# Splitting x and inverting row sums: high parts a step ahead of low parts, in a fused attention and two-MoE kernel

## The chip, the cores and the metric

The kernel runs on one core of a Trainium2 chip. The metric is the device time of one execution in microseconds (us), lower is better.

## The reference, cut to what matters

```python
def _attn_ref(q, k, v):               # B, H, S, D = 4, 8, 576, 64
    scores = scale * np.matmul(q, k.transpose(0, 1, 3, 2))
    ...
    scores = np.where(mask, scores + bias[None], -1000000000.0)   # causal, window 128
    scores = scores - np.max(scores, axis=-1, keepdims=True)
    attn = np.exp(scores)
    attn = attn / (np.sum(attn, axis=-1, keepdims=True) + 1e-09)
    return np.matmul(attn, v)

def _moe_ref(x, w_in, w_out):         # 2304 tokens, 512 -> 2048 -> 512
    h = x @ w_in
    g = h * np.cos(h)
    return g @ w_out

def _moe2_ref(x, w_in, w_out):
    h = x @ w_in
    g = np.where(h >= 1, h, np.where(h <= -1, 0.0, (h + 1) ** 2 / 4))
    return g @ w_out
```

The output of attention is x of the first MoE layer, and its output is x of the second.

## The kernel before, in words

Three stages follow one another: attention, then the first MoE layer over four chunks of tokens, then the second over five. The matmuls of the MoE layers run on pairs of numbers: every fp32 value is held as a rounded high part (a cast to fp32r, on ACT) and a low part (value minus high part, `sub_lo`, on DVE or POOL), and each product is three matmuls: high by high, low by high, high by low.

**Attention** works on 36 pairs, one for every 256 tokens and two heads. A pair has two blocks j of 128 tokens. For a pair, `pe_s` (L236) puts the scores of both blocks into the PSUM banks y0 to y3; `scores` (L253) adds the distances and takes the row minimum on DVE (L263) and the exponentials with their sums on ACT (L270); `prepare` (L445) adds 1e-9 to the sums on POOL and `invert` (L448) takes their reciprocals on DVE, or does both on DVE with `add=True`; `normalise` (L273) multiplies on POOL; `pe_t` (L280) transposes on PE into banks h0 and h1; `copy_t` (L293) copies each bank to SBUF, on DVE or ACT by the table `PT`; `pe_v` (L304) multiplies by v into bank h2 or h3; `put_x` (L319) takes the result out as part of x.

The loop of `attention` (L464) is a software pipeline. Step k emits `pe_s` and `scores` of pair k+3, inverts pair k+2, normalises pair k+1 (in the steps below 1 it normalises pair k+2 at once), transposes and copies pair k, and takes out pair k-1. The order on PE, DVE, ACT, POOL and SP is the order in which the code emits; nothing reorders it, so a waiting instruction holds up all that stands behind it on its engine. Behind the loop the last five pairs, p0 to p4 (pairs 31 to 35), are written out by hand, and then the first MoE layer starts with `mm_a` (L360).

Some work of the MoE layer lies in the attention stage. `make(0)` (L169) emits one of the small pieces that turn 64-bit weights into fp32 and split them (L114, L125, L131, L135, L140 and an L81); nine of them go into the steps in `D_STEPS`, five behind p4's copies. The first chunk's x has two parts. Its second part, tokens 512 to 767 (pairs 8 to 11, taken out in steps 9 to 12), is split straight from PSUM in `put_x`:

```python
            ACT.copy(hi, p["vb"][:, 0:256])
            sub_lo(DVE, lo, p["vb"][:, 0:256], hi)
```

Its first part, tokens 0 to 511, four tiles x0 to x3 of 128 x 512, is split by `split_x` (L347) late in the stage: x0 in step 30, x1 in step 31, x2 and x3 among the hand-written last pairs. Slots for x come from a list of 17 (L194): `new_x` takes the one that has been free the longest, `free_x` puts one back. The low parts xl of x0 to x3 lie where the distances of the four head pairs lie during attention. In a profile all low parts have the line of `sub_lo`, L81.

Of the kernel before, what the change touches and what calls it, by code (L numbers as in the profile page):

```python
# [10 lines left out]
F32R = mybir.dt.float32r  # L11
# [32 lines left out]
def attention_moe_moe_kernel(  # L44
# [9 lines left out]
    ACT, DVE, POOL, PE, SP = nc.scalar, nc.vector, nc.gpsimd, nc.tensor, nc.sync  # L54
# [15 lines left out]
    def nm(s):  # L70
        uid[0] += 1
        return f"{s}{uid[0]}"

    def small(name, dtype=F32, shape=(128, 512)):
        return two.tile(list(shape), dtype, tag="s", name=nm(name), bufs=12)

    def f32(ap):
        return ap.bitcast(F32)

    def sub_lo(eng, out, full, hi):  # L80
        eng.tensor_tensor(out=out, in0=full, in1=f32(hi), op=ALU.subtract)  # L81
# [81 lines left out]
    def start(m):  # L163

        if not started[m]:
            started[m] = True
            next(making[m])

    def make(m):  # L169

        start(m)
        if next(making[m], making) is not making:
            made[m] += 1
# [19 lines left out]
    x_tiles = {}  # L193
    x_free = {512: list(range(17)), 256: list(range(4))}  # L194

    def new_x(w, dtype=F32):
        size = w if x_free[w] else 512
        slot = size, x_free[size].pop(0)
        return one.tile([128, size], dtype, tag=f"x{size}.{slot[1]}", name=nm("x"))[:, 0:w], slot

    def free_x(slot):
        x_free[slot[0]].append(slot[1])
# [3 lines left out]
    def x_lo(n):  # L206

        return one.tile([128, 512 if n < 4 else 256], F32R, tag=f"xl{n}", name=nm("xl"))
# [17 lines left out]
    def load(n, part=slice(0, 1024)):  # L226
        if n < len(pairs):
            p = pairs[n]
            if "ld" not in p:
                p["ld"] = ring.tile([128, 1024], F32, tag="wl" if n % 2 else "wh", name=nm("qkv"))  # L230
                p["left"] = [0, 1024]
            if part.start >= p["left"][0] and p["left"][0] < 1024:
                p["left"][0] = part.stop
                SP.dma_start(p["ld"][:, part], qkv[p["b0"] // 2, p["hp"], :, part])
# [38 lines left out]
    def normalise(p):  # L273
        for j in range(2):
            st, sc, w = p["st"], p["sc"][j], p["w"][j]
            POOL.tensor_tensor(  # L276
                out=sc[:, :, 0:w], in0=sc[:, :, 0:w],
                in1=st[:, 8 + 2 * j:10 + 2 * j].unsqueeze(2).to_broadcast([128, 2, w]), op=ALU.mult)

    def pe_t(p):  # L280
        p["tb"], p["pt"] = [], [None] * 2
        for j in range(2):
            nb = p["w"][j] // 128
            b = ps.tile([128, 512], F32, tag=f"h{j}", name=nm("pa"))
            for h in range(2):
                for i in range(nb):
                    c = (h * nb + i) * 128
                    PE.transpose(b[:, c:c + 128], p["sc"][j][:, h, i * 128:i * 128 + 128], ident)  # L288
            p["tb"].append(b)
# [3 lines left out]
    def copy_t(p, j, eng=None):  # L293
        p["pt"][j] = pt = small("pt")
        n = 2 * p["w"][j]
        if (eng or PT[copies[0] % len(PT)]) == "A":
            ACT.copy(pt[:, 0:n], p["tb"][j][:, 0:n])
        else:
            DVE.tensor_copy(pt[:, 0:n], p["tb"][j][:, 0:n])
        copies[0] += 1  # L300
# [3 lines left out]
    def pe_v(p):  # L304
        v_no[0] += 1
        p["vb"] = b = ps.tile([128, 512], F32, tag=f"h{2 + v_no[0] % 2}", name=nm("pa"))
        for j in range(2):
            nb = p["w"][j] // 128
            for i in range(nb):
                for h in range(2):  # L310
                    vc = 640 + (j + 2 - nb + i) * 128 + 64 * h
                    c = (h * nb + i) * 128
                    PE.matmul(b[64 * h:64 * h + 64, j * 128:j * 128 + 128],  # L313
                              lhsT=p["ld"][:, vc:vc + 64], rhs=p["pt"][j][:, c:c + 128],
                              start=(i == 0), stop=(i == nb - 1))

    evicted = [0]

    def put_x(p, eng=None):  # L319
        t0 = p["b0"] * 128  # L320
        o, w = max(a for a in all_parts if a[0] <= t0)
        if (o, w) == chunks[0]["parts"][1]:
            hi, slot = new_x(w, F32R)
            lo = x_lo(4 + p["hp"])
            chunks[0]["xs", 1, p["hp"]] = hi, lo, slot
            ACT.copy(hi, p["vb"][:, 0:256])
            sub_lo(DVE, lo, p["vb"][:, 0:256], hi)
            return
        if (o, p["hp"]) not in x_tiles:
            x_tiles[o, p["hp"]] = new_x(w)  # L330
        x = x_tiles[o, p["hp"]][0][:, t0 - o:t0 - o + 256]
        if (eng or XE[evicted[0] % len(XE)]) == "A":
            ACT.copy(x, p["vb"][:, 0:256])
        else:
            DVE.tensor_copy(x, p["vb"][:, 0:256])
        evicted[0] += 1
# [8 lines left out]
            free_x(c["xs", i, d][2])  # L345

    def split_x(c, i, ds):  # L347
        o, w = c["parts"][i]
        for d in ds:
            x, slot = x_tiles.pop((o, d))  # L350
            hi, hi_slot = new_x(w, F32R)
            lo = x_lo(4 * i + d)[:, 0:w]
            ACT.copy(hi, x)
            sub_lo(DVE, lo, x, hi)
            free_x(slot)
            c["xs", i, d] = hi, lo, hi_slot

    h_no = [-1]

# [85 lines left out]
    def prepare(p):  # L445
        POOL.tensor_scalar_add(p["st"][:, 4:8], p["st"][:, 4:8], 1e-9)

    def invert(p, add=False):  # L448
        if add:
            DVE.tensor_scalar_add(p["st"][:, 4:8], p["st"][:, 4:8], 1e-9)  # L450
        DVE.reciprocal(p["st"][:, 8:12], p["st"][:, 4:8])  # L451

    def attention():
        qk, v = slice(0, 640), slice(640, 1024)
        for part in (qk, v):
            for n in range(3):
                load(n, part)
        make_identity(nc, ident)
        make_dist8()
        DVE.memset(half, 0.5)  # L460
        DVE.memset(half_pi, TWO_PI / 4)
        np_ = len(pairs)
        c0 = chunks[0]
        for k in range(-AHEAD, np_ - AHEAD - 1):  # L464
            new = pairs[k + AHEAD]
            mid = pairs[k + AHEAD - 1] if k + AHEAD >= 1 else None
            nrm = pairs[k + AHEAD - 2] if k >= 2 else None
            cur = pairs[k] if k >= 0 else None
            old = pairs[k - 1] if k >= 1 else None
            if k > -AHEAD:  # L470
                load(k + AHEAD + 1)
                load(k + AHEAD + 2)
            if k == 0:
                pe_t(cur)
            pe_s(new)
            if k > 0:
                pe_t(cur)
            if old:
                pe_v(old)
            scores(new, 0)  # L480
            if k < 1 and mid:

                prepare(mid)
                invert(mid)
                normalise(mid)
            if cur:
                copy_t(cur, 0)
            if nrm:
                normalise(nrm)
            if k >= 1:  # L490
                prepare(mid)
            scores(new, 1)

            if k in D_STEPS:
                make(0)
            if k in (np_ - 6, np_ - 5):
                split_x(c0, 0, [k - (np_ - 6)])
            if k >= 1:
                invert(mid)
            if cur:  # L500
                copy_t(cur, 1)
            if k + 1 == D_STEPS[0]:
                start(0)
            if old:
                put_x(old)

        p0, p1, p2, p3, p4 = pairs[np_ - 5:]
        pe_s(p4)
        pe_t(p1)
        pe_v(p0)  # L510
        scores(p4, 0)
        copy_t(p1, 0, "D")
        normalise(p2)
        invert(p3, add=True)
        normalise(p3)
        copy_t(p1, 1, "A")
        scores(p4, 1)
        pe_t(p2)
        pe_v(p1)
        copy_t(p2, 0, "D")  # L520

        ACT.activation(half_pi2, half, AF.Sin)
        put_x(p0, "A")
        invert(p4, add=True)
        normalise(p4)
        copy_t(p2, 1, "D")
        pe_t(p3)
        pe_v(p2)
        split_x(c0, 0, [2])
        put_x(p1, "D")  # L530
        copy_t(p3, 0, "D")
        copy_t(p3, 1, "A")
        pe_t(p4)
        pe_v(p3)
        put_x(p2, "A")
        split_x(c0, 0, [3])
        copy_t(p4, 0, "D")
        copy_t(p4, 1, "A")
        make(0)
        make(0)  # L540
        pe_v(p4)
        put_x(p3, "A")
        for _ in range(D_TAIL - 2):
            make(0)
        put_x(p4, "A")
# [115 lines left out]
```

## Time and profile before

| what | value |
|---|---|
| median of 3 runs | 930.52 us (930.34 to 932.04) |
| the profiled execution, its own time | 930.21 us |
| its span, first to last instruction | 928.4 us |
| PE busy | 909.6 us (98%) |
| DVE, ACT, POOL busy | 551.6 (59%), 435.2 (47%), 120.8 us (13%) |
| chain that ended last | PE 79%, DVE 10%, ACT 8%, issue 2% |
| granted TensorE clock | 0.999 |
| start of the first MoE matmul | 127.84 us |

How to read it: the span is that of one profiled execution; 1.8 us of that execution's own time lie outside it. PE is busy 98% of the span, but this is a mean over an attention stage of 128 us and MoE stages of 800 us. The chain that ended last is followed back from the last instruction to whatever released each step; where it passes through DVE or ACT, PE was waiting for them.

### The profile page before, as it was taken

Reading aid. Unit: us, or ns where it says so; the run is one execution under the profiler, and the core shown is the slowest. Engines: PE = TensorE matmul, PEld = TensorE weight load, DVE = VectorE, ACT = ScalarE, POOL = GpSimd, SP = SyncE. Lnnn points to the kernel's source line nnn. Section 1 sums busy time; section 2 is a strip of 40 time slices with the busy share of each in tenths; the row PEclk is TensorE's granted clock in tenths of the full one; section 3 lists DMA queues with packets and bytes.
Section 4 is the critical chain, followed back from the end, with each engine's and each line's share of the span. In section 5 each row is a group of like instructions: output and inputs, shape, how many; then the busy total and the mean of one; then the engine's idle time right before and its main releaser. Section 6 shows DMA issues by size and latency. Waiting matters only on the chain.

```text
span 928.4 us, 13106 instructions
## 1 busy us (share of the span) xinstructions
PE 909.6 (98%) x4944; PEld 755.2 (81%) x4944; DVE 551.6 (59%) x1192; ACT 435.2 (47%) x923; POOL 120.8 (13%) x147
## 2 busy tenths in 40 slices
PE   7999988999999999999999999999999999999998
PEld 5767777888888888888888888888888888888898
DVE  6888788888868667767433543344344334433443
ACT  7788865665655444444455532232233223322332
POOL 5666620000000000000144510000000000000000
PEclk9999999999999999999999999999999999999999
DMA  9346013333305443542322200010001000100100
GB/s 355 145 168 265 2 67 116 116 128 120 116 34 191 136 151 122 170 137 92 102 100 104 69 1 1 0 46 1 1 1 45 1 1 1 46 0 1 39 9 23
DMA packets 24687, 74.77 MB, mean 81 GB/s; under 512 B 2736, under 2 KB 3632, under 8 KB 24624
## 3 DMA queue, kind: packets, MB, share of 16 engines
q1 hardware_dynamic: 24624, 73.94, 22.9%
q8 instruction: 39, 0.64, 0.3%
q14 instruction: 24, 0.20, 0.1%
HBM read 60.82 MB, written 13.11 MB: 80 GB/s over the span
## 4 chain that ended last, share of the span: by engine, by line
PE 79%; DVE 10%; ACT 8%; issue 2%; POOL 0%; DMA 0%; ACTq 0%; DVEq 0%
PE y L425 36%; PE h L375 36%; PE pa L248 2%; PE pa L288 2%; PE pa L313 2%; DVE wu L131 2%; ACT t L391 2%; ACT sc L270 2%; DVE t L393 1%; ACT wh L140 1%; DVE wl L81 1%; DVE gl L81 1%; DVE wu L135 1%; ACT wu L114 1%; ACT gh L405 1%
## 5 line engine op out<-in xcount | busy, mean ns | idle before, releaser
L375 PE MATMUL h<-x,wh 128*128 128x512 f32 (+1 forms) x640 | 237.0, 370 | 1.0
L375 PE MATMUL h<-xl,wh 128*128 128x512 f32 (+1 forms) x640 | 235.6, 368 | 0.0
L375 PE MATMUL h<-x,wl 128*128 128x512 f32 (+1 forms) x640 | 235.5, 368 | 0.0
L425 PE MATMUL y<-gl,wh 128*128 128x512 f32 (+1 forms) x576 | 217.5, 378 | 0.4 <-DVE gl L81 0.4
L425 PE MATMUL y<-gh,wh 128*128 128x512 f32 (+1 forms) x576 | 217.3, 377 | 0.0
L425 PE MATMUL y<-gh,wl 128*128 128x512 f32 (+1 forms) x576 | 217.3, 377 | 0.0
L396 ACT ACTIVATE t<-t,half 128x512 f32<-128x512 f32 (+1 forms) x80 | 54.4, 680 | 189.7 <-DVE t L395 189.4
L375 PEld LDWEIGHTS h<-x,wh 128*128 128x128 f32 x640 | 120.6, 188 | 23.6 <-DVE t L393 3.2
L375 PEld LDWEIGHTS h<-x,wl 128*128 128x128 f32 x640 | 120.7, 189 | 20.3
L375 PEld LDWEIGHTS h<-xl,wh 128*128 128x128 f32 x640 | 120.6, 188 | 20.1
L81 DVE TENSOR_TENSOR gl<-t,gh 128x512 fp32r<-128x512 f32 (+1 forms) x144 | 95.5, 663 | 68.3 <-ACT gh L405 64.1
L405 ACT CAST gh<-t 128x512 fp32r<-128x512 f32 (+1 forms) x144 | 86.0, 597 | 105.0 <-DVE t L398 56.4
L425 PEld LDWEIGHTS y<-gl,wh 128*128 128x128 f32 x576 | 108.5, 188 | 21.0 <-DVE gl L81 1.1
L425 PEld LDWEIGHTS y<-gh,wh 128*128 128x128 f32 x576 | 108.4, 188 | 20.0
L425 PEld LDWEIGHTS y<-gh,wl 128*128 128x128 f32 x576 | 108.3, 188 | 19.9
L395 DVE TENSOR_SCALAR t<-h 128x512 f32<-128x512 f32 (+1 forms) x80 | 50.9, 636 | 88.9 <-PE h L375 88.8
L81 POOL TENSOR_TENSOR wl<-wst,wh 128x512 fp32r<-128x512 f32 x32 | 41.1, 1308 | 372.6 <-ACT wh L182 372.6
L398 DVE TENSOR_TENSOR t<-h,t 128x512 f32<-128x512 f32 (+1 forms) x80 | 51.1, 638 | 61.8 <-ACT t L396 61.8
L391 ACT ACTIVATE t<-t,half_pi 128x512 f32<-128x512 f32 x80 | 54.6, 682 | 62.6 <-DVE t L389 62.6
L389 DVE SCALAR_TENSOR_TENSOR t<-h,k 128x512 f32<-128x512 f32 x80 | 50.8, 635 | 54.6 <-ACT k L387 54.4
L270 ACT ACTIVATE sc<-sc,st 128x256 f32<-128x256 f32 (+1 forms) x144 | 70.2, 489 | 23.9 <-DVE st L263 20.5
L276 POOL TENSOR_TENSOR sc<-sc,st 128x512 f32<-128x512 f32 (+1 forms) x72 | 70.0, 994 | 35.3 <-DVE st L451 30.5
(56 smaller groups left out, 853.1 us busy)
## 6 DMA issues: line engine op xcount, KB each, us to landing
wst<-in_w SPq DMA_DIRECT2D x64, 512.0 KB, 3.7
qkv<-in_qkv SPq DMA_DIRECT2D x33, 512.0 KB, 9.4
wd<-wu SPq DMA_DIRECT2D x32, 256.0 KB, 2.4
wst<-wd SPq DMA_DIRECT2D x16, 512.0 KB, 3.3
out_t<-ys SPq DMA_DIRECT2D x16, 256.0 KB, 2.1
qkv<-in_qkv SPq DMA_DIRECT2D x3, 320.0 KB, 3.6
qkv<-in_qkv SPq DMA_DIRECT2D x3, 192.0 KB, 5.1
out_t<-ys SPq DMA_DIRECT2D x4, 128.0 KB, 1.8
```

The costliest lines, as they stand in the source:

```text
L81: eng.tensor_tensor(out=out, in0=full, in1=f32(hi), op=ALU.subtract)
L131: DVE.scalar_tensor_tensor(out=ui, in0=high, scalar=0x80000000, in1=ui, op0=ALU.bitwise_and, op1=ALU.bitwise_or)
L270: ACT.activation(sc[:, h, 0:w], sc[:, h, 0:w], AF.Exp, bias=st[:, c:c + 1], scale=-1.0, accum_out=st[:, 4 + c:5 + c])
L276: POOL.tensor_tensor(out=sc[:, :, 0:w], in0=sc[:, :, 0:w], in1=st[:, 8 + 2 * j:10 + 2 * j].unsqueeze(2).to_broadcast([128, 2, w]), op=ALU. ...
L375: PE.matmul(h, lhsT=a[:, 0, s], rhs=x, start=(n == 0), stop=(n == 11))
L389: DVE.scalar_tensor_tensor(out=t, in0=h, scalar=INV_2PI, in1=k, op0=ALU.mult, op1=ALU.subtract)
L391: ACT.activation(t, t, AF.Sin, bias=half_pi, scale=TWO_PI)
L395: DVE.tensor_scalar(out=t, in0=h, scalar1=-1.0, scalar2=1.0, op0=ALU.max, op1=ALU.min)
L396: ACT.activation(t, t, AF.Square, bias=half, scale=0.5)
L398: DVE.tensor_tensor(out=t, in0=h, in1=t, op=ALU.max)
L405: ACT.copy(gh, t)
L425: PE.matmul(c["y", i][d], lhsT=a[:, 1, s], rhs=x, start=(f == 0 and k == 0 and not (i and d % 2)), stop=(f == NF - 1 and k == 2 and (i == ...
```

## The change

Three edits. (1) In steps -2 to 0 the reciprocals of pairs 0 to 2 move from ahead of the second half of the new pair's scores to behind it; the addition of 1e-9 for them moves from POOL to DVE, and `normalise` follows there. (2) The low parts of pairs 8 to 11 are emitted on DVE one step later than the high parts on ACT, behind the next pair's scores. (3) x0, x1 and x2 get their high parts at the ends of steps 29, 30 and 31; the low parts of x0 and x1 follow in steps 30 and 31 behind the scores, and those of x2 and x3 move behind the copies of p4. One `make(0)` moves ahead of these copies.

```diff
--- before.py
+++ after.py
@@ -315,6 +315,7 @@
                               start=(i == 0), stop=(i == nb - 1))
 
     evicted = [0]
+    low_parts = []
 
     def put_x(p, eng=None):
         t0 = p["b0"] * 128
@@ -324,7 +325,7 @@
             lo = x_lo(4 + p["hp"])
             chunks[0]["xs", 1, p["hp"]] = hi, lo, slot
             ACT.copy(hi, p["vb"][:, 0:256])
-            sub_lo(DVE, lo, p["vb"][:, 0:256], hi)
+            low_parts.append(lambda: sub_lo(DVE, lo, p["vb"][:, 0:256], hi))
             return
         if (o, p["hp"]) not in x_tiles:
             x_tiles[o, p["hp"]] = new_x(w)
@@ -345,15 +346,23 @@
             free_x(c["xs", i, d][2])
 
     def split_x(c, i, ds):
+        for d in ds:
+            split_hi(c, i, d)()
+
+    def split_hi(c, i, d):
+
         o, w = c["parts"][i]
-        for d in ds:
-            x, slot = x_tiles.pop((o, d))
-            hi, hi_slot = new_x(w, F32R)
+        x, slot = x_tiles.pop((o, d))
+        hi, hi_slot = new_x(w, F32R)
+        ACT.copy(hi, x)
+
+        def rest():
             lo = x_lo(4 * i + d)[:, 0:w]
-            ACT.copy(hi, x)
             sub_lo(DVE, lo, x, hi)
             free_x(slot)
             c["xs", i, d] = hi, lo, hi_slot
+
+        return rest
 
     h_no = [-1]
 
@@ -478,11 +487,6 @@
             if old:
                 pe_v(old)
             scores(new, 0)
-            if k < 1 and mid:
-
-                prepare(mid)
-                invert(mid)
-                normalise(mid)
             if cur:
                 copy_t(cur, 0)
             if nrm:
@@ -493,17 +497,23 @@
 
             if k in D_STEPS:
                 make(0)
-            if k in (np_ - 6, np_ - 5):
-                split_x(c0, 0, [k - (np_ - 6)])
-            if k >= 1:
-                invert(mid)
+            while low_parts:
+                low_parts.pop()()
+            if mid:
+                invert(mid, add=k < 1)
+                if k < 1:
+
+                    normalise(mid)
             if cur:
                 copy_t(cur, 1)
             if k + 1 == D_STEPS[0]:
                 start(0)
             if old:
                 put_x(old)
-
+            if k >= np_ - 7:
+                low_parts.append(split_hi(c0, 0, k - (np_ - 7)))
+
+        x2, = low_parts
         p0, p1, p2, p3, p4 = pairs[np_ - 5:]
         pe_s(p4)
         pe_t(p1)
@@ -526,20 +536,21 @@
         copy_t(p2, 1, "D")
         pe_t(p3)
         pe_v(p2)
-        split_x(c0, 0, [2])
         put_x(p1, "D")
         copy_t(p3, 0, "D")
         copy_t(p3, 1, "A")
         pe_t(p4)
         pe_v(p3)
         put_x(p2, "A")
-        split_x(c0, 0, [3])
+        make(0)
         copy_t(p4, 0, "D")
         copy_t(p4, 1, "A")
+        x2()
+        pe_v(p4)
+        x3 = split_hi(c0, 0, 3)
+        put_x(p3, "A")
         make(0)
-        make(0)
-        pe_v(p4)
-        put_x(p3, "A")
+        x3()
         for _ in range(D_TAIL - 2):
             make(0)
         put_x(p4, "A")
```

On DVE at the program's start, steps -1 and 0 (`sc` are scores of a pair, `pa` the PSUM bank, `st` a pair's sums; `ISA` on sc is the addition with the row minimum, the row that follows reads its result), one piece of the difference:

```order
-L451 RECIPROCAL st_134<-st_134 128x4
-L263 ISA sc_177,st_159<-pa_164,xl_105 128x256
+L263 ISA sc_173,st_159<-pa_164,xl_105 128x256
 L263 ISA st_159 128x1
-L263 ISA sc_177,st_159<-pa_165,xl_105 128x256
+L263 ISA sc_173,st_159<-pa_165,xl_105 128x256
 L263 ISA st_159 128x1
+L459 TENSOR_SCALAR st_134<-st_134 128x4
+L460 RECIPROCAL st_134<-st_134 128x4
```

The reciprocal of the pair before (`st_134`) stood between the two halves of the next pair's scores; now both halves come first, then an addition, then the reciprocal.

On DVE around step 10 (`xl_674` is the low part of pair 8, `x_673` its high part from ACT, made at the end of step 9; `sc_707` here and `sc_716` below are scores of pair 13, `wu` a piece of weights), before:

```order
L131 SCALAR_TENSOR_TENSOR wu_355<-wst_353,wu_355 128x512
L451 RECIPROCAL st_573<-st_573 128x4
L81 TENSOR_TENSOR xl_674<-pa_645,x_673 128x256
L263 ISA sc_707,st_679<-pa_680,xl_102 128x256
L263 ISA st_679 128x1
```

and now:

```order
L263 ISA sc_716,st_678<-pa_684,xl_102 128x256
L263 ISA st_678 128x1
L81 TENSOR_TENSOR xl_674<-pa_645,x_673 128x256
L460 RECIPROCAL st_626<-st_626 128x4
L263 ISA sc_758,st_730<-pa_731,xl_105 128x256
```

The low part `xl_674` stood ahead of the first scores of pair 13 (`sc_707`); now it stands behind the last of them, ahead of the next reciprocal.

On DVE at the end of the stage, from the second copy of p2 on (`pt` are the copies of p2, p3 and p4, `xl` the low parts of x2 and x3, `wu` pieces of weights), before:

```order
L299 COPY pt_1876<-pa_1853 128x512
L81 TENSOR_TENSOR xl_1898<-x_357,x_1897 128x512
L335 COPY x_1692<-pa_1858 128x256
L299 COPY pt_1902<-pa_1878 128x512
L81 TENSOR_TENSOR xl_1927<-x_410,x_1926 128x512
L299 COPY pt_1930<-pa_1906 128x512
L131 SCALAR_TENSOR_TENSOR wu_1037<-wst_404,wu_1037 128x512
L135 SCALAR_TENSOR_TENSOR wu_1037<-wst_404,wu_1037 128x512
```

and now:

```order
L299 COPY pt_1878<-pa_1855 128x512
L336 COPY x_1692<-pa_1860 128x256
L299 COPY pt_1900<-pa_1880 128x512
L131 SCALAR_TENSOR_TENSOR wu_1037<-wst_404,wu_1037 128x512
L299 COPY pt_1925<-pa_1904 128x512
L81 TENSOR_TENSOR xl_1929<-x_357,x_1800 128x512
L135 SCALAR_TENSOR_TENSOR wu_1037<-wst_404,wu_1037 128x512
L81 TENSOR_TENSOR xl_1949<-x_410,x_1940 128x512
```

Ahead of the last copy two low parts are gone and one piece of weights has come; the low parts follow the last copy.

## Rows read from the trace of the kernel before

**Rows 1.** By stage: window, length, busy us of PE, PEld, DVE, ACT, POOL, clock, DMA, GB/s

```profile
127.84:150.00 22.16, 19.61 (x107) 16.62 (x106) 18.05 (x34) 12.92 (x26) 0.00 (x0) 1.00 0.35 119
```

**Rows 2.** Waits in 0 to 130 us: who waited for whom, us in total, times, longest

```profile
DVE xl L81 <- ACT x L326: 4.7, 4, 1.5
...
DVE xl L81 <- ACT x L353: 3.5, 3, 1.4
PE pa L288 <- DVE pt L299: 3.3, 3, 1.5
...
DVE st L451 <- POOL st L446: 2.7, 4, 1.0
```

**Rows 3.** Timeline at the start, PE: start us, duration, instruction xcount [idle before <- releaser]

```profile
9.39 0.66 PE L288 MATMUL pa<-ident,sc 128*128 128x128 f32 x4 [0.31 <-POOL sc L276]
...
12.78 1.04 PE L248 MATMUL pa<-qkv 64*128 64x256 f32 x4 [1.01 <-DVE st L263]
...
14.46 0.63 PE L288 MATMUL pa<-ident,sc 128*128 128x128 f32 x4 [0.28 <-ACT pt L297]
```

**Rows 4.** The same timeline, POOL

```profile
9.94 1.61 POOL L276 TENSOR_TENSOR sc<-sc,st 128x256 f32<-128x256 f32 x2 [0.30 <-DVE st L451]
11.64 0.22 POOL L446 TENSOR_SCALAR st<-st 128x4 f32<-128x4 f32 x1
```

**Rows 5.** The same timeline, DVE

```profile
11.89 0.18 DVE L451 RECIPROCAL st<-st 128x4 f32<-128x4 f32 x1 [0.88 <-POOL st L446]
...
12.30 0.41 DVE L263 CUSTOM_DVE_ANT_0 sc<-pa,xl 128x256 f32<-128x256 f32 x1
```

**Rows 6.** Timeline of steps 10 and 11, DVE: low parts of pairs 9 and 10

```profile
46.24 0.42 DVE L81 TENSOR_TENSOR xl<-pa,x 128x256 fp32r<-128x256 f32 x1 [1.46 <-ACT x L326]
...
50.81 0.42 DVE L81 TENSOR_TENSOR xl<-pa,x 128x256 fp32r<-128x256 f32 x1 [0.90 <-ACT x L326]
```

**Rows 7.** Timeline, PE: `pe_s` of pairs 13, 18 and 19

```profile
41.00 1.13 PE L248 MATMUL pa<-qkv 64*128 64x256 f32 x8
...
59.79 0.92 PE L248 MATMUL pa<-qkv 64*128 64x256 f32 x8
...
62.69 0.92 PE L248 MATMUL pa<-qkv 64*128 64x256 f32 x8
```

**Rows 8.** Timeline, PE: a full step (pairs 33, 30 and 29), then the end of attention

```profile
106.83 1.13 PE L248 MATMUL pa<-qkv 64*128 64x256 f32 x8
107.90 1.09 PE L288 MATMUL pa<-ident,sc 128*128 128x128 f32 x8
...
109.94 1.13 PE L248 MATMUL pa<-qkv 64*128 64x256 f32 x8
...
116.91 0.63 PE L288 MATMUL pa<-ident,sc 128*128 128x128 f32 x4 [1.49 <-DVE pt L299]
...
124.95 1.07 PE L288 MATMUL pa<-ident,sc 128*128 128x128 f32 x8 [1.46 <-DVE pt L299]
...
127.84 0.50 PE L375 MATMUL h<-x,wh 128*128 128x512 f32 x1
...
130.47 0.39 PE L375 MATMUL h<-x,wl 128*128 128x512 f32 x1
```

**Rows 9.** Timeline of the end, DVE

```profile
115.40 0.69 DVE L81 TENSOR_TENSOR xl<-x,x 128x512 fp32r<-128x512 f32 x1 [1.32 <-ACT x L353]
...
120.20 0.70 DVE L450 TENSOR_SCALAR st<-st 128x4 f32<-128x4 f32 x1 [0.28 <-ACT sc L270]
...
122.50 1.37 DVE L81 TENSOR_TENSOR xl<-x,x 128x512 fp32r<-128x512 f32 x1 [0.81 <-ACT x L353]
```

**Rows 10.** Timeline of the end, ACT

```profile
109.72 0.51 ACT L270 ACTIVATE sc<-sc,st 128x256 f32<-128x256 f32 x1 [0.53 <-DVE st L263]
...
110.72 0.60 ACT L353 CAST x<-x 128x512 fp32r<-128x512 f32 x1
```

**Rows 11.** Timeline of the end, POOL: the two halves of p4's `normalise`

```profile
121.28 2.04 POOL L276 TENSOR_TENSOR sc<-sc,st 128x512 f32<-128x512 f32 x2 [0.41 <-DVE st L451]
```

## The prediction

> **What bounds the kernel now.** First the table by stage. In the first 22 us of the MoE stage PE is busy 19.61 of 22.16 us [rows 1], and over the whole span 98%, so nearly all that attention loses, the kernel loses: what counts is how early the first MoE matmul, now at 127.84 us [rows 8], can start. The TensorE clock stands at its upper level throughout (granted 1.00 [rows 1]), so it is no term here. Next I read the PE timeline of attention for its undisturbed pace. A full step (`pe_s`, `pe_t`, `pe_v`) goes from 106.83 to 109.94, 3.11 us, without a wait of PE [rows 8]; one with a block of 128 keys goes from 59.79 to 62.69, 2.90 us [rows 7]. Third, the list of waits up to 130 us, for what breaks this pace [rows 2]: DVE waits 4.7 us, in four places, for the high parts of pairs 8 to 11; 3.5 us, in three, for those of x0, x1 and x2; 2.7 us, in four, for POOL's addition ahead of a reciprocal; PE waits 3.3 us, in three, for DVE copies. All are in-order waits: a DVE instruction stands at the head of its queue until ACT or POOL is done, with scores and copies ready behind it. Each of the three edits takes away one such group, so I cost three places.
>
> **Place one, the start.** In step 0 the reciprocal of pair 2 waits 0.88 us on DVE and starts at 11.89, since POOL's addition for it (11.64) stands behind a `normalise` of 1.61 us that began at 9.94 [rows 4, 5]. Behind it stand a copy and the second scores of pair 3 (12.30) [rows 5]; PE waits 1.01 us for these banks (12.78), then 0.28 us for ACT's copy (14.46) [rows 3], and from there runs at its pace. With the change those scores don't wait for POOL. The gain is at most the 1.01 us of PE's wait. Something comes off: the reciprocal of pair 0 now stands behind two scores (0.41 us each, overlapping [rows 5]), where it had waited anyway, and its `normalise`, on which PE waits 0.31 us at 9.39 [rows 3], comes about 0.2 us later. So 0.88 - 0.1 = **0.8 us**, nearest to the wait that goes. Bounds 0.4 and 1.0: the lower takes a further 0.4 us for an addition on DVE that meets a running `normalise`. The three new additions work on four numbers a partition (the one beside a running `normalise` took 0.70 us [rows 9]), and three on POOL go.
>
> On that price a row and a rule meet. The addition at 120.20 took 0.70 us, and the low part of x2 at 122.50 took 1.37 against 0.69 for that of x1 [rows 9], which began when POOL was idle; POOL's `normalise` ran from 121.28 to 123.32 [rows 11]. The Trainium skill (SBUF — State Buffer, "Who interferes with whom") says that a VectorE instruction with two SBUF inputs, or in a mode with two ports, is blocked until a GpSimd instruction that began first has ended. The long low part agrees: it ended 0.55 us after the `normalise`. By that rule the addition for pair 1, at about 9.1, would wait for pair 0's `normalise` until 9.5, and the sum would be 0.4 us smaller; by an addition that nothing holds up it would not.
>
> **Place two, steps 9 to 12.** Here the chain is a loop through two engines: the low part at the head of a DVE step waits for the high part on ACT (1.46 and 0.90 us in the rows shown [rows 6], 4.7 in all four [rows 2]), ACT's next exponentials wait for the scores behind that low part, and the next high part stands behind those exponentials. From `pe_s` of pair 13 to that of pair 18 five steps take 59.79 - 41.00 = 18.79 us [rows 7]. With the low part behind the next pair's four scores its high part is long done; the loop is open and the largest of three loads sets the step. PE: 3.11, or 2.90 for the last one. DVE: in the heaviest step, with a piece of weights and two copies, from 46.24 to the next low part at 50.81, less its 0.90 idle, 3.67 us [rows 6]. ACT was idle beside DVE's low part and the scores behind it, so I take it as no larger than PE. So 3 x 3.11 + 3.67 + 2.90 = 15.9, and the gain is 18.79 - 15.9 = **2.9 us**. Bounds: 3.2 if the heavy step hides in its neighbours' slack; 1.7 if the four steps keep 0.3 us each of new cross-waits. The low parts now hold their PSUM bank half a step longer; two banks alternate, and the next `pe_v` into the same one comes over a step later, so this costs nothing unless steps fall below 2 us.
>
> **Place three, the end.** From `pe_s` of pair 34 (109.94) to the first MoE matmul (127.84) there are 17.90 us [rows 8]. PE's own work: two full steps (6.22), three times `pe_t` and `pe_v` (3.11 - 1.07 = 2.04 each, 6.12; `pe_s` is the 1.07 from 106.83 to 107.90 [rows 8]) and one more `pe_v` (half of 2.04): 13.4 us. So PE stands for 4.5 us, among it 1.49 at 116.91 and 1.46 at 124.95, both for DVE copies behind low parts [rows 8]. What the change takes off DVE ahead of these copies: the wait for x0's high part, 1.4, and x1's, 1.32; for x2's 0.81 and its 1.37; and x3's low part, about 0.7 like x1's (a piece of weights takes a place there, but while DVE waits for p4's transposes) [rows 2, 9]. What then ends last: p4's exponentials, addition, reciprocal and copy of p2 (still in this order on ACT and DVE, with ACT's table load behind the exponentials), and POOL's `normalise` of p4, 2.04 us [rows 11], ahead of p4's transposes. These keep some 1.0 us of PE's stand, the size of the smaller waits there. 4.5 - 1.0 = **3.5 us**. Bounds 2.0 (the two large stalls, 2.95, less 1.0 for new ones) and 4.0.
>
> What is moved here and costs nothing as long as its cover holds: the high parts of x0 to x2 stand a step earlier on ACT, ahead of the next exponentials. At 109.72 ACT had been idle 0.53 us, and a high part takes 0.60, the end of it overlapping the next instruction [rows 10]: it just fits. Without that idle each delays exponentials by some 0.5 us. x3's high part takes the slot that x2's low part frees, so it now waits for DVE, with p3's `put_x`, a weight piece and p4's `put_x` behind it on ACT; ACT has nearly 3 us until the first h of the MoE stage is ready (12 matmuls, from 127.84 to 130.47 and the length of the last [rows 8]). The low parts of x2 and x3 must be there for the 8th and 11th of these matmuls, 1.7 and 2.4 us after the start (spacing 2.63 / 11 = 0.24 us [rows 8]); by the moved order I put their end about 0.5 us behind it. Weight pieces keep their order, and those behind the last copy start as much earlier as PE does. SP issues the same transfers in the same order; those of weights wait for DVE's pieces and move with them.
>
> **Sum.** 0.8 + 2.9 + 3.5 = 7.2 us, bounds 4.1 and 8.2. Against the profiled execution's own 930.21 us (span 928.4) this gives 923.0; the median of the runs, 930.52, stands 0.3 above that one, so I forecast **923.3 us**, with 922.3 to 926.4 as this case's own range.
>
> **The rivals.**
> 1. ACT takes over the loop. In steps 9 to 12 the high part waits for PE's `pe_v`, with the next exponentials behind it on ACT; if that wait is long, ACT is late in place of DVE. For it: ACT held low parts up by 0.90 and 1.46 us [rows 6]. Against: the idle times of ACT that the removed waits caused. Then place two gives half, 1.4: sum 5.7, **924.8 us**.
> 2. The end's gain is not passed on. If the first MoE steps hang on something that does not come earlier, PE starts sooner and stands longer: it already stands 22.16 - 19.61 = 2.5 us in its first 22 [rows 1]. Against: what it waits for there are DVE and ACT pieces that move with the start. Then 0.8 + 2.9 = 3.7: **926.8 us**.
> 3. Slower: the high parts become the bound on ACT. Seven of them come ahead of the next exponentials: three of 0.60 us [rows 10] and four with half as many numbers, some 0.3 each, 3.0 us. If in these steps ACT has no idle time once DVE stops waiting, each is paid in full, and the copies wait for ACT as they now wait for DVE, so that nothing is won but the start: 930.5 + 3.0 - 0.8 = **932.7 us**. It decides where ACT's idle per step falls under a high part's length; 0.53 at 109.72 [rows 10] stands against it, narrowly.
> 4. Other waits end just behind those removed, and nothing moves: **930.5 us**. The lengths of the waits speak against it: several behind them would all have to be hidden.
>
> **How the numbers follow.** My forecast has 0.77, rival 1 0.10, rival 2 0.05, rival 3 0.03, rival 4 0.05. A measurement of this kernel tells about 0.2%, 1.9 us, from no change. Faster by more: 0.77 + 0.10 + 0.05 = 0.92; within it 0.05; slower 0.03. The range runs from 922.0, just under the upper bound of the gain, to 926.9, which takes in rivals 1 and 2; left out are a larger gain than the bounds and rivals 3 and 4.
>
> **What would show it.** The first MoE matmul at about 120.6 us instead of 127.84, and all behind it earlier by the same. The list of waits without its rows of DVE for the high parts L326 and L353, the additions at the start on DVE below 0.2 us, PE's half `pe_t` of 14.46 at about 13.7, `pe_s` of pair 18 at about 56.1, and the way from `pe_s` of pair 34 to the MoE stage 14.4 us long. I am wrong if ACT shows waits for PE ahead of high parts with DVE idle behind them (rival 1), if the MoE starts early but PE's stand there grows (rival 2), or if ACT runs without idle and copies come later (rival 3).

## The result, and the profile after

| | before | changed |
|---|---|---|
| median of 4 runs | 931.25 us (930.34 to 932.04) | 923.09 us (922.73 to 924.59) |
| the profiled execution, its own time | 930.21 us | 922.75 us |
| its span | 928.4 us | 921.0 us |
| first MoE matmul starts | 127.84 us | 120.30 us |
| from there to the end of the span | 800.56 us | 800.70 us |

The ratio is 0.9916, with a 95% interval of 0.9899 to 0.9933. A second comparison, of 5 runs with 9 of before, gave 0.9912 (0.9898 to 0.9926), medians 922.97 and 930.56 us. The change makes the kernel faster by 0.8 to 0.9%, clear of the noise, as both intervals end below 1. 923.3 us was forecast, in a range of 922.0 to 926.9.

The three places, read from the PE timeline of the changed kernel:

```profile
9.88 0.66 PE L288 MATMUL pa<-ident,sc 128*128 128x128 f32 x4 [0.56 <-POOL sc L276]
...
13.91 0.63 PE L288 MATMUL pa<-ident,sc 128*128 128x128 f32 x4 [0.28 <-ACT pt L297]
...
40.45 1.13 PE L248 MATMUL pa<-qkv 64*128 64x256 f32 x8
...
46.67 1.14 PE L248 MATMUL pa<-qkv 64*128 64x256 f32 x8
...
50.02 0.92 PE L248 MATMUL pa<-qkv 64*128 64x256 f32 x8
...
53.25 0.92 PE L248 MATMUL pa<-qkv 64*128 64x256 f32 x8
...
56.15 0.92 PE L248 MATMUL pa<-qkv 64*128 64x256 f32 x8
...
106.32 1.13 PE L248 MATMUL pa<-qkv 64*128 64x256 f32 x8
...
115.80 0.63 PE L288 MATMUL pa<-ident,sc 128*128 128x128 f32 x4 [0.37 <-DVE pt L299]
...
117.38 1.09 PE L288 MATMUL pa<-ident,sc 128*128 128x128 f32 x8
...
120.30 0.50 PE L384 MATMUL h<-x,wh 128*128 128x512 f32 x1
```

Against [rows 3, 7, 8] the reader sees: PE's wait of 1.01 us for the scores' banks at 12.78 is gone, and the half `pe_t` of pair 1 starts at 13.91 in place of 14.46. Here PE's first matmul came at 4.02, with its first transfer, 0.14 us later than before, so the start gave 0.69 us. From `pe_s` of pair 13 (40.45) to that of pair 18 (56.15) there are 15.70 us in place of 18.79: 3.09 us. Up to `pe_s` of pair 34 nothing more changes (50.17 us in place of 50.15). From there (106.32) to the first MoE matmul there are 13.98 us in place of 17.90: 3.92 us, and of the stalls of 1.49 and 1.46 us one of 0.37 is left. 0.69 + 3.09 + 3.92 = 7.70, less the later first transfer and 0.02, is the 7.54 us by which the MoE stage starts earlier. All of it but 0.14 us is in the span.

In the list of waits up to 125 us of the changed kernel the rows of [rows 2] are gone or small; these stand in their place (waiting and waited for, us, times, longest):

```profile
ACT x L357 <- DVE xl L81: 0.4, 1, 0.4
PE pa L288 <- DVE pt L299: 0.4, 1, 0.4
...
DVE st L460 <- POOL st L455: 0.2, 1, 0.2
```

No low part waits for a high part any more. The first row is the new wait that was announced, x3's high part for the slot of x2. The chain that ended last went to and fro between ACT and DVE in steps 9 to 12 of the kernel before (start, us, what):

```profile
45.95 0.28 ACT x L326
...
46.24 0.42 DVE xl L81
...
48.33 1.09 ACT sc L270 x4
...
50.51 0.28 ACT x L326
```

In the changed kernel it stays on PE there:

```profile
40.52 1.06 PE pa L248 x8
41.58 1.02 PE pa L288 x8
42.61 1.02 PE pa L313 x16
43.63 1.06 PE pa L248 x8
```

The first 22.16 us of the MoE stage, by stage as in [rows 1]:

```profile
120.30:142.46 22.16, 19.61 (x96) 16.53 (x95) 18.86 (x35) 13.45 (x27) 0.00 (x0) 0.92 0.37 119
```

PE is busy 19.61 us, as before, but at a lower clock (0.92) and with fewer matmuls in the window (x96 against x107; see the last section), so this row alone proves little. A later execution of the changed kernel, with the clock at 1.00, has both figures of before:

```profile
120.60:142.76 22.16, 19.61 (x107) 16.61 (x106) 18.85 (x35) 13.34 (x27) 0.00 (x0) 1.00 0.37 119
```

With the 800.56 and 800.70 us from the first MoE matmul to the end of the span, the MoE stage has moved as a whole.

### The profile page after: what moved, and what is told of

Read it like the earlier page. It is cut to its first block, busy times and chain, and to the rows that moved or that the text cites. A ratio compares the mean times of both kernels' runs of the same rounds, so it can differ in the third digit from the quotient of the medians.

```text
span 921.0 us, 13111 instructions
## 1 busy us (share of the span) xinstructions
PE 906.8 (98%) x4944; PEld 754.6 (82%) x4944; DVE 552.9 (60%) x1195; ACT 434.8 (47%) x923; POOL 120.4 (13%) x144
## 4 chain that ended last, share of the span: by engine, by line
PE 83%; DVE 8%; ACT 7%; issue 2%; DMA 0%; POOL 0%; ACTq 0%; DVEq 0%; POOLq 0%
PE y L434 36%; PE h L384 36%; PE pa L248 4%; PE pa L288 4%; PE pa L313 3%; DVE wu L131 2%; ACT t L400 2%; ACT wh L140 1%; DVE t L402 1%; DVE wl L81 1%; DVE gl L81 1%; DVE wu L135 1%; ACT gh L414 1%; ACT wu L114 1%; ACT sc L270 1%
```

## The experiments

The theory: three separate in-order waits were removed, each worth what PE had stood for it, independent of one another. Times of one profiled execution are given by place, so that a start that differs by some tenths does not matter.

### One edit at a time

**Start alone.** The kernel before, with only this:

```diff
-            if k < 1 and mid:
-                prepare(mid)
-                invert(mid)
-                normalise(mid)
...
-            if k >= 1:
-                invert(mid)
+            if mid:
+                invert(mid, add=k < 1)
+                if k < 1:
+                    normalise(mid)
```

> Only the first edit, reciprocals of pairs 0 to 2 behind the next scores with their additions on DVE; the rest as before. Order theory (each removed wait gives its own gain, whatever the others do): PE's half transposes of pair 1 at about 13.9 us (14.46 before), first MoE matmul at about 127.2 us (127.84), time lower by 0.6 us than that of the kernel before. Rival (a start that is earlier is swallowed by the steps 9 to 12, where DVE and ACT wait for each other): half transposes at 13.9, first MoE matmul at 127.8, time unchanged.

Measured: half `pe_t` of pair 1 at 13.94, first MoE matmul at 127.30, time 929.66 us where the runs of before had a median of 930.36. PE's first matmul came at 4.04 in place of 3.88, so the gain is 0.68 us at the half `pe_t` and 0.70 at the first MoE matmul: all of it arrives there. The rival falls: steps 9 to 12 carry an earlier start through, since what binds there is a loop of durations, not a fixed date.

**Steps 9 to 12 alone.** The kernel before, with only this:

```diff
+    low_parts = []
...
-            sub_lo(DVE, lo, p["vb"][:, 0:256], hi)
+            low_parts.append(lambda: sub_lo(DVE, lo, p["vb"][:, 0:256], hi))
...
+            while low_parts:
+                low_parts.pop()()
             if k in (np_ - 6, np_ - 5):
                 split_x(c0, 0, [k - (np_ - 6)])
```

> Only the second edit, low parts of pairs 8 to 11 a step later, behind the next scores; the rest as before. Order theory: from the scores matmuls of pair 13 to those of pair 18 about 15.7 us (18.79 before, 15.70 with the whole change), first MoE matmul at 124.7 us, time about 3.1 us lower, 927.1 where before takes 930.2. Rival (these steps gain only because the stage around them is opened too): more than 17 us from pair 13 to 18, under 2 us gained.

Measured: median 927.3 us of 7 runs, ratio 0.9969 (0.9958 to 0.9980). PE timeline, `pe_s` of pairs 13 and 18:

```profile
42.57 1.13 PE L248 MATMUL pa<-qkv 64*128 64x256 f32 x8
...
58.26 0.92 PE L248 MATMUL pa<-qkv 64*128 64x256 f32 x8
```

That is 15.69 us, as with the whole change. The first MoE matmul came at 126.30, not at 124.7: this execution (928.58 us, above the median) had lost 1.5 us to a slower clock before 18 us (last section). The list of waits still has 3.5 us for x0 to x2, and none for pairs 8 to 11.

**End alone.** The changed kernel with the first two edits undone:

```diff
-            low_parts.append(lambda: sub_lo(DVE, lo, p["vb"][:, 0:256], hi))
+            sub_lo(DVE, lo, p["vb"][:, 0:256], hi)
...
+            if k < 1 and mid:
+                prepare(mid)
+                invert(mid)
+                normalise(mid)
...
-            if mid:
-                invert(mid, add=k < 1)
-                if k < 1:
-                    normalise(mid)
+            if k >= 1:
+                invert(mid)
```

> Only the third edit, high parts of x0 to x2 a step sooner and low parts of x2 and x3 behind the last copies; the rest as before. Order theory: from the scores matmuls of pair 34 to the first MoE matmul about 14.0 us (17.90 before, 13.98 with the whole change), first MoE matmul at 124.0 us, time about 3.9 us lower, 926.3 where before takes 930.2. Rival (the end's gain needs the earlier places): above 15.5 us, under 2.5 us gained. If the three gains of these runs add up to the 7.5 us of the whole change, the places are independent.

Measured: median 927.83 us of 6 runs (926.31 to 928.13), ratio 0.9965 (0.9953 to 0.9978). PE timeline, `pe_s` of pair 34 and the first MoE matmul:

```profile
111.67 1.13 PE L248 MATMUL pa<-qkv 64*128 64x256 f32 x8
...
125.66 0.50 PE L384 MATMUL h<-x,wh 128*128 128x512 f32 x1
```

13.99 us, as with the whole change. The median is 1.5 us above the time expected. The traced execution (927.91 us) had the slower clock before 18 us, as in the run above; for the others only the mean clock is known, and it fits: 0.996 in all four of 927.77 to 928.13 us, 0.998 in the two of 926.31 and 926.53. The lowest of the six, 926.31, is 3.9 us under the lowest of before, 930.25. By place the three edits give 0.70, 3.10 and 3.91 us, together 7.71, where the whole change gives 7.70 by place: the places are independent.

### What of the start is order, and what is the engine

The changed kernel, with the additions back on POOL:

```diff
             if mid:
-                invert(mid, add=k < 1)
                 if k < 1:
+                    prepare(mid)
+                invert(mid)
+                if k < 1:
                     normalise(mid)
```

> The whole change, but the three additions of 1e-9 stay on POOL, ahead of the reciprocal that follows the scores. Order theory (the gain of the start comes from putting the scores ahead of the wait): half transposes of pair 1 at 13.9 to 14.2 us, first MoE matmul at 120.3 to 120.6 us. Rival (the gain comes from taking the additions off POOL, where they stand behind a normalise): half transposes at about 14.5, first MoE matmul at about 120.9 us, 0.6 us of the change lost.

Measured: PE's first matmul at 3.91, half `pe_t` of pair 1 at 13.53, first MoE matmul at 119.90; time 922.23 us, one run. PE timeline:

```profile
13.53 0.63 PE L288 MATMUL pa<-ident,sc 128*128 128x128 f32 x4 [0.28 <-ACT pt L297]
```

Theory and rival both expected it later. Counted from PE's first matmul, the half `pe_t` comes at 9.62 us, against 9.89 with the whole change and 10.58 before. So the order alone is worth 0.96 us, nearly all of the 1.01 us that PE had waited, and the additions on DVE cost 0.27 of it. The DVE timeline of the run with the start alone shows what an addition meets there:

```profile
7.70 0.17 DVE L450 TENSOR_SCALAR st<-st 128x4 f32<-128x4 f32 x1
...
9.08 0.79 DVE L450 TENSOR_SCALAR st<-st 128x4 f32<-128x4 f32 x1
9.90 0.18 DVE L451 RECIPROCAL st<-st 128x4 f32<-128x4 f32 x1
11.01 0.29 DVE L263 CUSTOM_DVE_ANT_0 sc<-pa,xl 128x128 f32<-128x128 f32 x1 [0.93 <-PE pa L248]
```

and POOL's there:

```profile
8.23 1.61 POOL L276 TENSOR_TENSOR sc<-sc,st 128x256 f32<-128x256 f32 x2 [5.71 <-DVE st L451]
```

Alone an addition takes 0.17 us; the one that meets POOL's `normalise` lasts 0.79, to 9.87, just after that `normalise` ends at 9.84. That one has cover, as DVE then waits 0.93 us for PE's next scores. The other has none: on DVE it stands ahead of the reciprocal on which pair 0's `normalise` waits, and PE awaits that. This `normalise` starts at 8.21 in the changed kernel (POOL):

```profile
8.21 1.61 POOL L276 TENSOR_TENSOR sc<-sc,st 128x256 f32<-128x256 f32 x2 [5.67 <-DVE st L460]
```

and at 7.83 with the addition on POOL:

```profile
7.83 1.61 POOL L276 TENSOR_TENSOR sc<-sc,st 128x256 f32<-128x256 f32 x2 [0.36 <-DVE st L460]
```

### The two halves of the end

**New order behind the loop, x0 and x1 split as before:**

```diff
+            if k in (np_ - 6, np_ - 5):
+                split_x(c0, 0, [k - (np_ - 6)])
             if mid:
...
-            if k >= np_ - 7:
-                low_parts.append(split_hi(c0, 0, k - (np_ - 7)))
+            if k == np_ - 5:
+                low_parts.append(split_hi(c0, 0, 2))
```

> The whole change, but x0 and x1 are split in steps 30 and 31 as before, high and low part together; the end behind the loop keeps the new order. Order theory: the two waits of 1.4 and 1.32 us come back, and with them PE's stall of 1.5 us; what the new order behind the loop gives stays. From the scores matmuls of pair 34 to the first MoE matmul about 16 us (17.90 before, 13.98 with the whole change). Rival (only the order behind the loop counts, since PE can catch up there): about 14 us.

Measured, PE timeline:

```profile
106.66 1.13 PE L248 MATMUL pa<-qkv 64*128 64x256 f32 x8
...
113.62 0.63 PE L288 MATMUL pa<-ident,sc 128*128 128x128 f32 x4 [1.49 <-DVE pt L299]
...
123.06 0.50 PE L384 MATMUL h<-x,wh 128*128 128x512 f32 x1
```

16.40 us from `pe_s` of pair 34, 2.42 more than with the whole change; the first stall of 1.49 us is back, and two waits of DVE for x0 and x1, 2.7 us together.

**x0 and x1 as changed, the order behind the loop as before:**

```diff
-            if k >= np_ - 7:
+            if np_ - 7 <= k < np_ - 5:
...
         pe_v(p2)
+        split_x(c0, 0, [2])
...
-        make(0)
+        split_x(c0, 0, [3])
         copy_t(p4, 0, "D")
         copy_t(p4, 1, "A")
-        x2()
+        make(0)
+        make(0)
         pe_v(p4)
-        x3 = split_hi(c0, 0, 3)
         put_x(p3, "A")
-        make(0)
-        x3()
```

> The whole change, but behind the loop the order of before: x2 and x3 are split among the copies of p3 and p4; x0 and x1 keep the high parts a step ahead. Order theory: PE's second stall of about 1.5 us ahead of p4's transposes stays, and about 2 us are lost against the whole change: from the scores matmuls of pair 34 to the first MoE matmul about 15.9 us. Rival (the waits in the loop are all that counts): about 14 us.

Measured, PE timeline:

```profile
106.56 1.13 PE L248 MATMUL pa<-qkv 64*128 64x256 f32 x8
...
119.15 1.06 PE L288 MATMUL pa<-ident,sc 128*128 128x128 f32 x8 [1.46 <-DVE pt L299]
...
122.04 0.50 PE L384 MATMUL h<-x,wh 128*128 128x512 f32 x1
```

15.48 us, 1.50 more than with the whole change, and the second stall of 1.46 us is back. 2.42 + 1.50 = 3.92 us: the two halves make up the end's gain exactly. Both rivals fall.

### Has ACT become the bound?

Every high part of the first chunk is made twice in the changed kernel:

```diff
         ACT.copy(hi, x)
+        if (c["m"], i) == (0, 0) and c is chunks[0]:
+            ACT.copy(hi, x)
...
             ACT.copy(hi, p["vb"][:, 0:256])
+            ACT.copy(hi, p["vb"][:, 0:256])
```

> The whole change, with each of the eight high parts made twice on ACT, one copy behind the other: 4 x 0.28 and 4 x 0.5 us more ACT work in the places where the high parts now stand. Order theory (ACT has idle time there and PE sets the pace): first MoE matmul later by 0.3 to 1.5 us than the 120.3 us of the whole change; the step from pair 13 to pair 18 at most 0.5 us longer than 15.70. Rival 3 (ACT is the bound once DVE no longer waits): each copy is paid in full, first MoE matmul later by 1.1 us in steps 9 to 12 and by 1.5 us at the end, 2.6 us in all.

Measured: time 923.28 us, one run; first MoE matmul at 120.88, 0.58 us later than with the change, or 0.72 counted from PE's first matmul (3.88 against 4.02). Busy time from `pe_s` of pair 13 to that of pair 18, PE, PEld, DVE, ACT, POOL, in this run:

```profile
40.33:56.17 15.84, 15.52 (x162) 11.93 (x160) 14.39 (x60) 15.00 (x54) 11.35 (x15) 1.00 0.51 190
```

and in the changed kernel:

```profile
40.45:56.15 15.70, 15.52 (x163) 11.95 (x161) 14.35 (x60) 14.13 (x51) 11.44 (x15) 1.00 0.50 188
```

ACT is busy 0.87 us more, and the stage is 0.14 us longer: PE stays the bound there, at 15.52 us busy in both, with ACT now close behind (15.00 of 15.84). At the end the way from `pe_s` of pair 34 takes 14.55 us in place of 13.98; there ACT has little left, and PE waits 0.69 us for one of its copies. Of some 3 us of added work 0.7 is paid. Rival 3 is refuted for this change, but another 0.5 us of ACT work per step at the end would not be free.

### What is still to be had

The changed kernel again, beside two versions:

> The changed kernel as it is, timed beside the next two. Expected: 922.8 us where before takes 930.3, ratio 0.992; most runs within 0.5 us of each other and some 1.3 to 1.5 us above.

Measured: 922.97 us (922.70 to 923.66). All five runs lie within 1.0 us; none came 1.3 to 1.5 us above the others.

**Weight pieces elsewhere, additions on POOL.**

```diff
-D_STEPS = (4, 9, 11, 13, 14, 15, 16, 18, 20)
+D_STEPS = (4, 9, 11, 13, 14, 15, 19, 21, 24)
...
-                invert(mid, add=k < 1)
                 if k < 1:
+                    prepare(mid)
+                invert(mid)
+                if k < 1:
                     normalise(mid)
```

> The whole change with the three additions back on POOL and the last three weight pieces of the loop moved from steps 16, 18 and 20 to 19, 21 and 24. Order theory: the additions on DVE cost 0.3 us at the start, and the step of 3.79 us from pair 20 to pair 21, in which ACT's and DVE's weight pieces hold up the copies, comes near 2.7 to 3.1: first MoE matmul at about 119.4 us, time about 921.9, 0.9 us under the changed kernel. Rival (the weight pieces cost the same wherever they stand): about 922.4.

Measured: median 922.37 us (921.47 to 922.50), first MoE matmul at 119.99. In the changed kernel ACT's copy of a pair waits behind two weight pieces of step 16 (ACT timeline):

```profile
62.78 0.68 ACT L114 ACTIVATE wu<-wst 128x512 f32<-128x512 f32 x1
63.36 0.61 ACT L140 CAST wh<-wu 128x512 fp32r<-128x512 f32 x1
63.87 0.37 ACT L297 COPY pt<-pa 128x256 f32<-128x256 f32 x1
```

and `pe_s` of pairs 20 and 21 are 61.73 and 65.53, 3.8 us apart. With the pieces moved (PE timeline):

```profile
62.15 1.13 PE L248 MATMUL pa<-qkv 64*128 64x256 f32 x8
64.84 1.20 PE L248 MATMUL pa<-qkv 64*128 64x256 f32 x8
```

2.69 us. Not all of the 1.1 us stays: step 21 becomes longer, and from pair 18 to pair 34 the stage is shorter by 0.73 us (49.44 in place of 50.17). The profiled execution lost some 0.9 us at the start: `pe_s` of pair 13 came 37.02 us after PE's first matmul, against 36.16 in the run above that has the additions on POOL and the same start. The weight loads of `pe_s` up to 16 us took 330 ns in the median (235 in the changed kernel), with the granted clock at 1.00, and DVE waited 1.42 us for PE's scores of pair 3; hence 119.99 and not 119.4. Why these loads were slow stays open.

**x1's low part behind the last copies too.** As above, with

```diff
-            while low_parts:
+            while low_parts and k < np_ - 5:
...
-            if k >= np_ - 7:
+            if np_ - 7 <= k < np_ - 5:
...
-        x2, = low_parts
+        x1, = low_parts
...
-        x2()
+        x1()
+        x2 = split_hi(c0, 0, 2)
         pe_v(p4)
+        make(0)
+        x2()
...
-        make(0)
         x3()
```

> As the run before, and x1's low part also moves behind the last copies; x2's high part follows there, since its slot comes from x1. Order theory: x1's low part (0.6 us) stands ahead of DVE's copy for pair 31 and on the way to the end; without it first MoE matmul 0.5 us earlier still, about 118.9 us, time about 921.4. Rival (the chain of low part, slot and high part is too long, the MoE matmuls that need x3 wait): no gain, with a stand of PE of 0.3 to 1 us in the first twelve MoE matmuls.

Measured: median 921.88 us (921.68 to 922.44), first MoE matmul at 119.04. From `pe_s` of pair 34 to there are 13.58 us, 0.40 less than with the change, and little over the 13.4 of PE's own work. The first twelve MoE matmuls run from 119.04 to 121.67 at their old pace, so x3 comes in time for them and the rival falls as it was put. The MoE matmuls start 1.26 us earlier than with the change; from there to the end of the span are 801.06 us in place of 800.70, so 0.9 us is left in the span. The trace shows where most of the other 0.36 us is lost: DVE waits 0.93 us for x3's high part, what stands behind its low part on DVE comes later in the MoE stage, and PE then waits for the first `gl` (DVE, then PE):

```profile
120.53 0.69 DVE L81 TENSOR_TENSOR xl<-x,x 128x512 fp32r<-128x512 f32 x1 [0.93 <-ACT x L357]
...
127.08 0.50 PE L434 MATMUL y<-gl,wh 128*128 128x512 f32 x1 [0.30 <-DVE gl L81]
```

This matmul comes 8.04 us after the first MoE matmul, in the changed kernel 7.58 (127.88). So the rival's long chain seems to cost something, only later than it said; no run separates it. All 4 runs lie under all 5 of the changed kernel, by 1.1 us in the median; at 0.12% that is below what a single measurement tells, and it rests on the places in the trace.

## Why the prediction was right

- **The bound.** The step that carried the rest held: what attention gains, the whole kernel gains. 7.54 us at the start of the MoE stage became 7.4 in the span and 7.46 in the execution's time. The MoE stage kept its length (800.70 us in place of 800.56 to the end of the span) and its own 2.5 us of PE's stand, so rival 2 did not come.
- **Place one**, 0.8 forecast, 0.69 measured. The mechanism was right: the order is worth 0.96 of the 1.01 us. What comes off was placed rightly, at pair 0's `normalise`, but under-sized and put down to the wrong cause. The prediction had it 0.2 us later, for the scores ahead of its reciprocal. Counted from PE's first matmul it starts at 3.85 us in the kernel before (7.73), at 3.92 with the order alone and at 4.19 with the additions on DVE. So the order delays it by 0.07, and the addition of pair 0, which the sum had at nothing, by 0.27; that is the whole difference between 0.96 and 0.69. The addition for pair 1 met POOL's `normalise`, as the rule of the Trainium skill has it that was weighed there (SBUF — State Buffer, "Who interferes with whom"), and the rows show it: 0.79 us with the start alone, 0.31 in the changed kernel, in place of 0.17, until POOL's instruction had ended. So the sign that the additions at the start stay below 0.2 us failed for this one. But the 0.4 us that the sum was to lose by this were not lost: behind it DVE stood 0.93 us for PE's next scores in both.
- **Place two**, 2.9 forecast, 3.09 measured. The mechanism was right, one step was counted wrongly. Two of the five steps, not one, have a block of 128 keys (`pe_s` of 0.92 us at 50.02 and 53.25), so PE's own load is 3 x 3.11 + 2 x 2.90 = 15.13 us. With this the forecast's own terms, 2 x 3.11 + 3.67 + 2 x 2.90, give 15.69, and 15.70 was measured. By step it came as 3.11, 3.11, 3.35, 3.23 and 2.90: the 0.56 us by which DVE's heavy step exceeds PE's was paid in full, 0.24 in that step and 0.33 in the next. That all of it is DVE's load is argued from the equal sums; no run separates it. The upper bound of 3.2, for a heavy step that hides in its neighbours, should by these loads have been 18.79 - 15.13 = 3.66; nothing hid.
- **Place three**, 3.5 forecast, 3.92 measured. PE's own 13.4 us were right. Of the stand 0.6 us is left, where 1.0 had been put. What was named as last there is last: the 0.37 us at 115.80 is the wait for DVE's copy behind p4's exponentials, addition and reciprocal. The chain shows more: that addition (DVE) met POOL's `normalise` of p3 and lasted until its end.

```profile
114.17 0.69 DVE L459 TENSOR_SCALAR st<-st 128x4 f32<-128x4 f32 x1 [0.24 <-ACT sc L270]
...
112.80 2.04 POOL L276 TENSOR_TENSOR sc<-sc,st 128x512 f32<-128x512 f32 x2 [0.46 <-DVE st L460]
```

  It took 0.69 us in place of 0.16, 0.53 more, and the stand behind it is 0.37. That the stand would go with it was not tried.
- **Costed at nothing.** The high parts ahead of the exponentials did cost nothing that the places show: ACT could take them twice for 0.7 us. x3's high part waited 0.37 us for its slot, and nobody waited for it: the low parts of x2 and x3 came on DVE at

```profile
118.75 0.68 DVE L81 TENSOR_TENSOR xl<-x,x 128x512 fp32r<-128x512 f32 x1
...
120.19 0.69 DVE L81 TENSOR_TENSOR xl<-x,x 128x512 fp32r<-128x512 f32 x1
```

  The second ends 0.58 us after the first MoE matmul (forecast: about 0.5), and the eleventh needs it 2.4 us after.
- **Rivals.** ACT did not take the loop over (1): the chain stays on PE, and steps 9 to 12 gave more than forecast. High parts did not become the bound (3). Nothing else ended just behind the removed waits (4).

The forecast median of 923.3 us is 0.2 above the measured one. Part of that closeness is luck: the terms were off by -0.1, +0.2 and +0.4 us, 0.5 together, and the median of before that the sum started from was 930.52, later ones 931.25, 930.36 and 930.56.

## What to carry to other kernels

On an engine that works in order, split a dependent pair of operations that lie on two engines: issue the first one a step ahead, and its consumer behind the work that is ready anyway; the gain is the idle time of whoever waits at the end of that queue, and where the waits lie in separate stages the gains add. Size it by the stage: when the loop through two engines is open, the new step is the largest of the engines' own loads. Count them step by step: here a single step in which another engine's load stood 0.56 us above PE's was paid in full, spread over two steps. A wait that is removed by moving work to another engine is not free: look at what runs beside it there.

## What the runs showed of the hardware that was not expected

- In 4 of the 12 profiled executions TensorE's granted clock falls to its lower level, 1.2 GHz, for some 3 to 4 us in the first 18 us. Clock from 14 to 18 us in the run with steps 9 to 12 alone (columns as in [rows 1]; the clock is the third from the end, 0.50 from 15 to 17 us), after a stretch from 12 to 14 us in which PE was busy 1.18 of 2 us:

```profile
12.00:14.00 2.00, 1.18 (x6) 0.79 (x6) 1.80 (x10) 1.32 (x7) 1.63 (x3) 1.00 1.01 406
14.00:18.00 4.00, 3.73 (x24) 2.75 (x24) 1.62 (x7) 2.81 (x10) 2.03 (x4) 0.57 1.03 407
```

  `pe_s` of pair 6 then came at 20.06 in place of 18.50, 1.5 us late, and this is the distance between that kernel's runs of about 927.2 and those of about 928.7. In the kernel before, PE was busy 1.22 of 2 us in the same stretch and the clock stayed at 1.00, so what decides stays open. In the two runs on the halves of the end, which have the new start, it fell between about 10.5 and 14 us and cost 0.3 to 0.4 us; there the changed kernel's chain runs over ACT's exponentials (11.32 to 13.30), not over PE. In the profiled execution of the changed kernel it fell from about 135 to 139 us, in the MoE stage, after PE had stood 2.4 us: that is the 0.92 above. The same fall stands behind the same wait in six other traces, and in five the clock stayed at 1.00 after it. There it cost nothing that can be seen: from the first MoE matmul to the end of the span an execution of the same kernel with the clock at 1.00 throughout took 800.6 us, this one 800.70.
- A DVE addition on 128 x 4 numbers took 0.16 to 0.17 us alone and up to 0.79 beside a running POOL instruction. A weight piece (L131), 0.69 us elsewhere, took 1.33 at 116.50 in the changed kernel, while POOL's last `normalise` ran; it stood ahead of the last copy and yet cost nothing, as DVE had to wait for p4's transposes.
